# A recurrence and a gated feed-forward in one kernel: another order of the opening, the range guard moved, and one input kept in 128 rows

## The chip, the cores and the metric

The kernel runs on one core of one Trainium2 chip. The metric is the device time of one execution in microseconds (us), taken as the median of several executions; lower is better. The engines are named as in the profile: PE (TensorE, the matrix engine), DVE (VectorE), ACT (ScalarE), POOL (GpSimd), SP (SyncE, which here only issues transfers). "PEld" is PE's loading of weights.

## What is computed

The reference has two parts, one after the other. The first is a linear recurrence over 768 tokens for 4 batches and 8 heads of 48 channels; the second is a feed-forward with a sigmoid gate over all 3072 tokens (384 channels in, 1536 hidden, 384 out), in float32:

```python
for t in range(S):                       # S = 768
    cur = np.einsum('bhd,bhe->bhde', u[None] * kt, vt)
    y[:, :, t] = np.einsum('bhd,bhde->bhe', rt, state + cur)
    state = wt[:, :, :, None] * state + np.einsum('bhd,bhe->bhde', kt, vt)
...
gate = 1.0 / (1.0 + np.exp(-(x @ w_gate)))
val = x @ w_val
return gate * val @ w_out                # x is y, reshaped to 3072 tokens
```

## The kernel before, in words

**Tiling.** Time is cut into six blocks of 128 tokens, and each block holds four groups, one per batch: 24 groups, numbered q = 0 to 23. For each group the recurrence is computed in closed form ("attention"): two scans over the decays on VectorE turn k and r into scaled k and r (`prep_k` L365, `prep_r` L384), matmuls make the products of k and r and the sums for the state (`pairs`, `from_state`, `sums`, `mix`), a bonus term with u runs on POOL (`bonus1` to `bonus4`), and transposes (`turn_x`) bring the result into the form x that the feed-forward reads. x is split into a high and a low part, each a tile of the type fp32r; weights and hidden values are split the same way, and three products stand for one float32 product.

**Inputs.** For each group two loads are issued on SP's queue: `pin` (`load_pin` L324: decays, k and r, one row for each of 112 lanes, 1544 words long; for group 0 in two pieces) and `tok` (`load_tok` L333: r, k and v by token, 128 rows). The weights lie in DRAM as float64 words; their 12 slices of the hidden dimension are fetched once (`fetch` L272, the tile is called wraw, a transfer of 1151.6 KB) and turned into float32 high and low parts in five operations: `w_top` on ACT (L281), `w_body` and `w_join` on DVE (L286, L290), `w_hi` on ACT (L313), `w_lo` on DVE (L316). In the text a slice is called a words, and p3, t3, w3 are the loads of pin 3, tok 3 and words 3; ub is the small load of u for all rows. The tiles pin and tok exist twice, so the load of a third group waits until the first has been used.

**The opening** is all that happens for blocks one and two: attention of groups 0 to 11 (and part of 12), all 12 words, and the feed-forward of the first two blocks, in units of half a block (256 tokens) by one slice. Its order is not written out. A planner (`Plan` L172, fed from L611 on) plays the program through at the time of building: each operation has an engine, an estimated cost, operations it must follow, buffers it takes and gives, and a rank; at each free engine the ready operation of lowest rank is emitted. The ranks of groups and words come from the list TURNS, those of the half blocks from LAGS (unit f of half block g has rank 100 + f + LAGS[g]). Loads on SP don't choose: they are emitted strictly in the order of the list COMES, and one that must wait for its buffer holds up all behind it. The costs only steer the order; on the chip semaphores decide when anything runs.

**Blocks three to six** have a fixed order (L712 to L743): for each block n, 4 times 3 steps (j, i), one for each slice f = 3j + i. A step is a gate (9 matmuls of 128x512), a value (9), and the down products of the step before (9); ACT makes the sigmoid and the high part hh, DVE the product and the low part hl. Between them lie the parts of the next block's attention, group by group, three steps to a group (`steps` L690): the step i = 1 ends with the transposes of x, the loads of the group after next and the first scan of the next. The last block (n = 5) has no attention beside it.

**The range guard.** The cheap way to turn the weights into float32 holds only within a range. So the kernel reads all weights a second time, in 36 pieces (three to a slice, 384 KB each, the tile is called seen), and ACT sums three functions of each piece (`w_guard` L301, three activations with an accumulator on L305, L306, L307). There is one buffer for the pieces: `see(g + 1)` (L294), called at the end of `w_guard(g)`, fetches the next piece on SP's queue once ACT has read the last. In blocks three to five a piece is handled in two of three steps (i = 1 and 2, right behind the sigmoid), 24 in all; the other 12 in the first six steps of block six, two in each step (one behind the sigmoid, one behind hh). `check_bounds` (L596) and `add_bounds` (L606) then turn the sums into a flag; if it were set, a slow general form would compute everything anew (`general` L49), which doesn't happen with these inputs.

Of the kernel before, what the change touches and what calls it, by code (L numbers as in the profile page):

```python
# [9 lines left out]
F32 = mybir.dt.float32  # L10
# [38 lines left out]
def general(ctx: ExitStack, tc: tile.TileContext, dec, tok, wts, u, out, ident):  # L49
# [47 lines left out]
    with tc.For_i(0, NC_) as c:  # L97
        for b in range(B):
            nc.sync.dma_start(d[:, b], decs[b, bass.ds(c, 1)].rearrange("o a w -> (o a) w"))
        with tc.For_i(0, C) as i:  # L100
# [71 lines left out]
class Plan:  # L172
# [8 lines left out]
    def run(self):  # L181
# [3 lines left out]
        while ends:  # L185
            now = min(ends)[0]
            for e in [e for e in ends if e[0] <= now]:
                ends.remove(e)
                if e[1] in self.ops:
                    for r in self.ops[e[1]][6]:  # L190
                        room[r] += 1
                    for n in left:
                        left[n].discard(e[1])
            moved = True
            while moved:
                moved = False
                for n in sorted((n for n in self.ops if n not in started and not left[n]), key=lambda n: self.ops[n][3]):
                    engine, cost, _, _, work, take, _ = self.ops[n]
                    if engine and free.get(engine, 0.0) > now or engine == "SP" and n != transfers[0]:
                        continue  # L200
                    if any(room[r] < take.count(r) for r in take):
                        continue
                    for r in take:
                        room[r] -= 1
                    if engine:
                        free[engine] = now + cost
                        ends.append((now + cost, "-" + n))
                    if engine == "SP":
                        transfers.pop(0)
                    ends.append((now + cost + (2.0 if engine == "SP" else 0.11 if engine else 0.0), n))  # L210
# [11 lines left out]
def tile_kernel(ctx: ExitStack, tc: tile.TileContext, dec: bass.AP, tok: bass.AP, wts: bass.AP, u: bass.AP, out: bass.AP):  # L222
# [101 lines left out]
    def load_pin(q):  # L324
        t = p2.tile([L, WW + 2 * NP * C], F32, tag="pin", name=f"pin{q}")
        if q == 0:
            nc.sync.dma_start(t[:, :WW], dec[place(q)][:, :WW])
            nc.sync.dma_start(t[:, WW:], dec[place(q)][:, WW:])
        else:
            nc.sync.dma_start(t, dec[place(q)])  # L330
        pin[q] = t

# [285 lines left out]

    add("ub", "SP", 0.6, [], comes["ub"], lambda: nc.sync.dma_start(ub, u.partition_broadcast(P)))
    for q in range(3 * B + 2):  # L620
        k = rank.get(f"c{q}", 99)
        add(f"pin{q}", "SP", 2.6, [], comes[f"p{q}"], load_pin, q, take=["pin"])
        add(f"tok{q}", "SP", 2.2, [], comes[f"t{q}"], load_tok, q, take=["tok"])
        if q > 3 * B:
# [4 lines left out]
        add(f"b4_{q}", "POOL", 1.45, [f"b3_{q}"], k, bonus4, q)  # L629
        add(f"pk{q}", "DVE", 2.18, [f"pin{q}"], k, prep_k, q, take=["eg"])  # L630
# [3 lines left out]
        add(f"pr{q}", "DVE", 2.12, [f"pk{q}"], k + 0.1, prep_r, q)  # L634
# [3 lines left out]
        add(f"tk{q}", "PE", 0.5, [f"pk{q}"], k + 0.1, turn_k, q, take=["bank", "kT"])  # L638
        add(f"kT{q}", "ACT", 0.52, [f"tk{q}"], k + 0.1, take_k, q, give=["bank"])
        add(f"sm{q}", "PE", 0.75, [f"kT{q}", f"tok{q}"], k + 0.15, sums, q, take=["bank", "bank"], give=["kT"])  # L640
        add(f"mid{q}", "DVE" if old else "ACT", 0.36, [f"sm{q}", old and f"fade{q}"], k + 0.12, middle, q, take=["mid"], give=["bank"])
        add(f"keep{q}", "DVE", 0.36, [f"mid{q}"], k + 0.15, keep, q, give=["bank"])
        add(f"sc{q}", "PE", 1.2, [f"pr{q}", f"mid{q}"], k + 0.2, scores, q, take=["bank", "bank", "at"], give=["pin"] + ["ready"] * old)
        add(f"m0{q}", "DVE", 0.43, [f"sc{q}"], k + 0.2, mask, q, 0)
        add(f"m1{q}", "DVE", 0.43, [f"m0{q}"], k + 0.2, mask, q, 1)
        add(f"mx{q}", "PE", 0.85, [f"m1{q}"], k + 0.3, mix, q, give=["at"])
# [4 lines left out]
        add(f"tx{q}", "PE", 0.42, [f"y1{q}", q % B and f"tx{q - 1}"], k + 0.4, turn_x, q, take=["bank"] + ["x"] * first, give=["bon"])  # L651
        add(f"xh{q}", "ACT", 0.68, [f"tx{q}"], k, take_x, q)
        add(f"xl{q}", "DVE", 0.57, [f"xh{q}"], k, rest_x, q, give=["bank"])
        add(f"tok{q}done", None, 0, [f"mx{q}", f"sm{q}", f"b4_{q}", q % B and f"tok{q - 1}done"], k, give=["tok"])
    for f in range(NFF):
        k = rank[f"w{f}"]
        add(f"words{f}", "SP", 4.1, [], comes[f"w{f}"], fetch, f)
        add(f"wg{f}", "ACT", 1.29, [f"words{f}"], k, w_top, f)
        add(f"wb{f}", "DVE", 0.83, [f"words{f}", f and f"wb{f - 1}"], k, w_body, f, take=["full"])
        add(f"wt{f}", "DVE", 1.39, [f"wb{f}", f"wg{f}"], k, w_join, f)  # L660
        add(f"wh{f}", "ACT", 1.15, [f"wt{f}"], k, w_hi, f)
        add(f"wl{f}", "DVE", 1.4, [f"wh{f}"], k, w_lo, f, give=["full"])
    for g, (n, i0, i1) in enumerate(GROUPS):
# [50 lines left out]
    for n in range(2, NC_):  # L714
        for j in range(B):
            trio = steps((n + 1) * B + j) if n + 1 < NC_ else nothing
            for i in range(3):
# [12 lines left out]
                hidden_hi(*a)  # L730
                if n == NC_ - 1 and j < 2:
                    w_guard(guarded)
# [49 lines left out]
```

## Time and profile before

| | |
|---|---|
| median of 3 timed runs | 596.22 us (596.21 to 597.75) |
| the profiled execution, its own time | 599.11 us |
| its span, first to last instruction | 597.3 us |
| mean granted clock of PE | 0.994 |
| busy: PE, DVE, ACT, POOL | 557.5, 320.1, 248.1, 96.0 us |
| bytes read and written in DRAM | 59.26 MB, 4.72 MB |

The profile is of one execution. Busy time is that of an engine's own instructions; the same time can be busy on several engines. For each instruction the trace knows what ended the idle time before it (a matmul of PE, a landed transfer, ...), and the "chain that ended last" follows these back from the end: whatever stands in the chain held up the end. A group row of the view by stretches gives the busy time of each engine in a stretch of the span, with the number of instructions in brackets. In the view of instructions in order of time, each row is the start, the length, engine, line and operation, the tile written, an arrow and the tiles read. Names of tiles as above; sg, hh, hl are the hidden values of a step, pg, pu, po the banks of gate, value and down products, pa, pv, pk, px those of attention.

### The profile page before, as it was taken

What the parts mean: (1) busy time and instruction counts of PE and PEld (TensorE: products, weight loads), DVE (VectorE), ACT (ScalarE), POOL (GpSimd) and SP (SyncE); (2) the same over time, 40 slices, a digit from 0 to 9 for tenths busy, and PEclk for the clock granted to TensorE, in tenths of its full rate; (3) what the DMA queues carried; (4) which work ended last, traced back from release to release, by engine and by line L of the source; (5) the groups of instructions that cost most, each with busy time, mean ns of one, the idle gap of its engine ahead of it and who ended that gap; (6) DMA issues with size and microseconds to landing.
All of it is one profiled execution on the core that took longest, in us unless ns stands there. A gap on an engine that the chain in (4) does not pass through costs nothing.

```text
span 597.3 us, 14497 instructions
## 1 busy us (share of the span) xinstructions
PE 557.5 (93%) x6330; PEld 478.3 (80%) x6330; DVE 320.1 (54%) x561; ACT 248.1 (42%) x577; POOL 96.0 (16%) x86
## 2 busy tenths in 40 slices
PE   3469899999999999899999999999999999988996
PEld 2358899999999999788888888888888888866785
DVE  3887988885458736254454454454454453111222
ACT  2455455443234213343443543443544343656411
POOL 3321502012111303011220220220220210000000
PEclk9999999999999999899999999999999999999998
DMA  8993609204331242143043243043244111333001
GB/s 228 289 325 113 245 28 314 71 3 126 100 91 47 87 136 67 54 140 112 30 140 115 80 140 114 27 140 115 86 134 115 43 38 38 126 102 105 27 1 57
DMA packets 16803, 64.95 MB, mean 109 GB/s; under 512 B 1904, under 2 KB 3312, under 8 KB 15200
## 3 DMA queue, kind: packets, MB, share of 16 engines
q1 hardware_dynamic: 14000, 59.66, 32.6%
q10 hardware_dynamic: 2736, 4.33, 2.0%
q8 instruction: 51, 0.84, 0.6%
q14 instruction: 16, 0.13, 0.1%
HBM read 59.26 MB, written 4.72 MB: 107 GB/s over the span
## 4 chain that ended last, share of the span: by engine, by line
PE 76%; DMA 13%; DVE 4%; ACT 4%; issue 1%; POOL 1%; ACTq 0%; SPq 0%; DVEq 0%; POOLq 0%
PE pu L523 22%; PE pg L523 21%; PE po L576 15%; PE po L558 6%; DMA seen<-wts 5%; DMA wraw<-wts 4%; PE pa L490 3%; DMA pin<-dec 3%; PE pa L419 2%; PE pa L429 2%; PE pk L402 1%; ACT sq L305 1%; PE pv L466 1%; PE px L502 1%; DVE full L290 1%
## 5 line engine op out<-in xcount | busy, mean ns | idle before, releaser
L523 PE MATMUL pg<-x,w 128*128 128x256 f32 (+1 forms) x864 | 170.0, 342 | 4.9 <-ACT sg L534 4.8
L523 PE MATMUL pu<-x,w 128*128 128x256 f32 (+1 forms) x864 | 172.2, 344 | 0.0
L523 PEld LDWEIGHTS pg<-x,w 128*128 128x128 f32 x864 | 137.7, 192 | 25.1 <-ACT sg L534 7.3
L523 PEld LDWEIGHTS pu<-x,w 128*128 128x128 f32 x864 | 136.9, 191 | 17.6 <-DVE sg L541 0.2
L541 DVE TENSOR_TENSOR sg<-pu,sg 128x256 f32<-128x256 f32 (+1 forms) x96 | 53.4, 557 | 137.7 <-PE pu L523 114.0
L534 ACT ACTIVATE sg<-pg 128x256 f32<-128x256 f32 (+1 forms) x96 | 46.9, 488 | 128.7 <-PE pg L523 126.8
L545 ACT CAST hh<-sg 128x256 fp32r<-128x256 f32 (+1 forms) x96 | 49.2, 512 | 107.9 <-DVE sg L541 107.2
L576 PE MATMUL po<-hh,w 128*128 128x512 f32 x288 | 89.3, 392 | 0.0
L549 DVE TENSOR_TENSOR hl<-sg,hh 128x256 fp32r<-128x256 f32 (+1 forms) x96 | 57.0, 594 | 52.3 <-ACT hh L545 52.2
L363 POOL TENSOR_TENSOR bon<-tok,a 128x384 f32<-128x384 f32 x24 | 33.2, 1382 | 247.3 <-DVE a L359 247.3
L576 PEld LDWEIGHTS po<-hh,w 128*128 128x128 f32 x288 | 54.0, 188 | 10.8
L576 PE MATMUL po<-hl,w 128*128 128x512 f32 x144 | 58.8, 408 | 0.6 <-DVE hl L549 0.5
L352 POOL TENSOR_TENSOR bon<-tok,ub 128x384 f32<-128x384 f32 x24 | 33.6, 1400 | 143.2 <-DMA tok<-tok 54.9
L558 PE MATMUL po<-w,hh 128*128 128x384 f32 x192 | 48.9, 336 | 0.0
L497 DVE TENSOR_TENSOR bon<-pa,bon 128x192 f32<-128x192 f32 x48 | 15.5, 353 | 52.5 <-PE pa L490 52.3
L558 PE MATMUL po<-w,hl 128*128 128x384 f32 x96 | 33.6, 350 | 4.9 <-DVE hl L549 4.9
L397 ACT ACTIVATE junk<-eg 112x1032 bf16<-112x1032 f32 x24 | 25.5, 1064 | 26.6 <-DVE eg L387 26.5
L370 DVE TENSOR_TENSOR_SCAN eg<-pin,ends 112x516 f32<-112x516 f32 x24 | 31.2, 1298 | 9.5 <-DMA pin<-dec 9.5
L558 PEld LDWEIGHTS po<-w,hh 128*128 128x128 f32 x192 | 34.9, 188 | 0.0
L576 PEld LDWEIGHTS po<-hl,w 128*128 128x128 f32 x144 | 27.0, 188 | 7.7 <-DVE hl L549 2.4
L387 DVE TENSOR_TENSOR_SCAN eg<-pin,heads 112x516 f32<-112x516 f32 x24 | 29.9, 1246 | 0.0
L355 POOL TENSOR_TENSOR bon<-bon,tok 128x384 f32<-128x384 f32 x24 | 27.2, 1132 | 1.8
(73 smaller groups left out, 545.2 us busy)
## 6 DMA issues: line engine op xcount, KB each, us to landing
pin<-dec SPq DMA_DIRECT2D x23, 675.5 KB, 6.5
tok<-tok SPq DMA_DIRECT2D x24, 576.0 KB, 6.2
seen<-wts SPq DMA_DIRECT2D x36, 384.0 KB, 3.1
wraw<-wts SPq DMA_DIRECT2D x12, 1151.6 KB, 13.9
y<-o ACTq DMA_DIRECT2D x10, 256.0 KB, 2.0
y<-o ACTq DMA_DIRECT2D x8, 192.0 KB, 1.9
pin<-dec SPq DMA_DIRECT2D x1, 448.0 KB, 3.6
y<-o SPq DMA_DIRECT2D x1, 256.0 KB, 2.3
```

The costliest lines, as they stand in the source:

```text
L352: nc.gpsimd.tensor_tensor(out=bon[q], in0=tk[q][:, 0:DM], in1=ub, op=ALU.mult)
L355: nc.gpsimd.tensor_tensor(out=bon[q], in0=bon[q], in1=tk[q][:, DM:2 * DM], op=ALU.mult)
L363: nc.gpsimd.tensor_tensor(out=by_head(bon[q]), in0=by_head(tk[q][:, 2 * DM:]), in1=a0, op=ALU.mult)
L370: nc.vector.tensor_tensor_scan(out=e[:, 516:0:-1], data0=t[:, 516:0:-1], data1=ends[:, 516:0:-1], initial=0.0, op0=ALU.mult, op1=ALU.add,)
L387: nc.vector.tensor_tensor_scan(out=e[:, WW:WW + 516], data0=t[:, 0:516], data1=heads[:, 0:516], initial=0.0, op0=ALU.mult, op1=ALU.add,)
L523: nc.tensor.matmul(t, lhsT=w[f][:, cols], rhs=x[n][:, a, k, i0 * C:i1 * C], start=k == 0 and j == 0, stop=k == NKT - 1 and j == 2)
L534: nc.scalar.activation(sg, hid["g", n, f, i0], AF.Sigmoid)
L541: nc.vector.tensor_tensor(out=sg, in0=hid["u", n, f, i0], in1=sg, op=ALU.mult)
L545: nc.scalar.copy(hh, hid["s", n, f, i0])
L549: nc.vector.tensor_tensor(out=hl, in0=hid["s", n, f, i0], in1=hid["hi", n, f, i0].bitcast(F32), op=ALU.subtract)
L558: nc.tensor.matmul(po[n, i][:, :DM], lhsT=h[:, c], rhs=w[f][:, 2 * DM:], start=f == 0 and j == 0, stop=f == NFF - 1 and j == 2,)
L576: nc.tensor.matmul(po[n, k], lhsT=w[f][:, cols], rhs=h, start=f == 0 and j == 0, stop=f == NFF - 1 and j == 2)
```

## The change

Three edits, in one diff.

1. The opening's lists are other ones: TURNS, COMES, LAGS, and some of the planner's estimated costs (u 1.4 and not 0.6, pin 2.9 and not 2.6, words 3.7 and not 4.1, matmul work of the first three groups dearer, and others by a few hundredths). The engines' work in the opening is the same, in another order.
2. The range guard: in blocks three to five one piece in each of the 36 steps, behind hh; none in block six. The two steps that turn the sums into the flag move from slices 6 and 8 of block six to slices 0 and 3.
3. The array with decays, k and r has 128 rows for each group and not 112 (rows 112 to 127 are never used), and the tile pin and its load have 128 partitions; all that computes uses the first 112 as before.

```diff
-TURNS = "c5 c7 w10 c0 w8 w9 c1 c3 c8 w4 c4 w1 w7 w5 c11 w2 c6 c12 c10 w11 w6 c2 w0 w3 c9"
-COMES = "p0 t0 ub w0 p1 w1 t1 t3 p3 w2 w3 p2 w10 t2 w4 w5 t8 t4 w7 p4 w6 t5 w8 p5 w11 w9 p8 t6 t7 p6 t11 p7 t9 p9 p10 p11 t10 p13 t13 p12 t12"
+TURNS = "w10 c0 w6 c2 w1 c3 w0 c8 w3 c4 c1 c9 w7 c11 c7 w2 c6 w8 w11 w4 w5 c5 c12 c10 w9"
+COMES = "p0 t0 p1 ub w0 p2 t1 w1 t2 p3 w2 w3 w6 t3 w5 w4 w11 p4 t4 p5 w9 p6 t7 w7 t5 w10 w8 t6 t8 p7 p11 p8 t9 t11 p12 p9 p10 t10 t12 p13 t13"
-LAGS = [138.0, 318.0, 326.5, 116.0]
+LAGS = [96.5, 328.5, 417.5, 78.5]
...
     def load_pin(q):
-        t = p2.tile([L, WW + 2 * NP * C], F32, tag="pin", name=f"pin{q}")
+        t = p2.tile([P, WW + 2 * NP * C], F32, tag="pin", name=f"pin{q}")
...
-        pin[q] = t
+        pin[q] = t[:L]
...
                 sigmoid(*a)
-                if n < NC_ - 1 and i or n == NC_ - 1 and j < 2:
-                    w_guard(guarded)
-                    guarded += 1
...
                 hidden_hi(*a)
-                if n == NC_ - 1 and j < 2:
+                if n < NC_ - 1:
                     w_guard(guarded)
                     guarded += 1
...
-                if n == NC_ - 1 and j == 2 and i == 0:
+                if n == NC_ - 1 and j == 0 and i == 0:
                     check_bounds()
-                if n == NC_ - 1 and j == 2 and i == 2:
+                if n == NC_ - 1 and j == 1 and i == 0:
                     add_bounds()
...
-    dec = np.zeros((NG, L, WW + 2 * NP * C), np.float32)
-    dec[:, :, :NP * W1].reshape(NG, L, NP, W1)[..., 1:] = lanes(inputs["w"], 1.0)
+    dec = np.zeros((NG, P, WW + 2 * NP * C), np.float32)
+    for p in range(NP):
+        dec[:, :L, p * W1 + 1:(p + 1) * W1] = lanes(inputs["w"], 1.0)[:, :, p]
```

More of the change, by code (lines that the diff above doesn't have):

```diff
@@ L209, in run @@
                         transfers.pop(0)
-                    ends.append((now + cost + (2.0 if engine == "SP" else 0.11 if engine else 0.0), n))
+                    ends.append((now + cost + (2.0 if engine == "SP" else 0.13 if engine else 0.0), n))
                     started.add(n)
@@ L617, in add @@
         plan.add(name, engine, cost, after, rank, f and (lambda: f(*args)), take, give)
-    add("ub", "SP", 0.6, [], comes["ub"], lambda: nc.sync.dma_start(ub, u.partition_broadcast(P)))
+    add("ub", "SP", 1.4, [], comes["ub"], lambda: nc.sync.dma_start(ub, u.partition_broadcast(P)))
     for q in range(3 * B + 2):
         k = rank.get(f"c{q}", 99)
-        add(f"pin{q}", "SP", 2.6, [], comes[f"p{q}"], load_pin, q, take=["pin"])
-        add(f"tok{q}", "SP", 2.2, [], comes[f"t{q}"], load_tok, q, take=["tok"])
+        add(f"pin{q}", "SP", 2.9, [], comes[f"p{q}"], load_pin, q, take=["pin"])
+        add(f"tok{q}", "SP", 2.3 + 1.4 * (not q), [], comes[f"t{q}"], load_tok, q, take=["tok"])
         if q > 3 * B:
@@ L629, in tile_kernel @@
         add(f"b4_{q}", "POOL", 1.45, [f"b3_{q}"], k, bonus4, q)
-        add(f"pk{q}", "DVE", 2.18, [f"pin{q}"], k, prep_k, q, take=["eg"])
+        add(f"pk{q}", "DVE", 2.2, [f"pin{q}"], k, prep_k, q, take=["eg"])
         old = q >= B
@@ L637, in tile_kernel @@
             continue
[L638 removed]
+        add(f"tk{q}", "PE", 0.4 + 0.5 * (q < 3), [f"pk{q}"], k + 0.1, turn_k, q, take=["bank", "kT"])
         add(f"kT{q}", "ACT", 0.52, [f"tk{q}"], k + 0.1, take_k, q, give=["bank"])
[L640 removed]
+        add(f"sm{q}", "PE", 0.7 + 0.5 * (q < 3), [f"kT{q}", f"tok{q}"], k + 0.15, sums, q, take=["bank", "bank"], give=["kT"])
         add(f"mid{q}", "DVE" if old else "ACT", 0.36, [f"sm{q}", old and f"fade{q}"], k + 0.12, middle, q, take=["mid"], give=["bank"])
         add(f"keep{q}", "DVE", 0.36, [f"mid{q}"], k + 0.15, keep, q, give=["bank"])
[L643 removed]
+        add(f"sc{q}", "PE", 1.2 + 1.2 * (q < 3), [f"pr{q}", f"mid{q}"], k + 0.2, scores, q, take=["bank", "bank", "at"], give=["pin"] + ["ready"] * old)
         add(f"m0{q}", "DVE", 0.43, [f"sc{q}"], k + 0.2, mask, q, 0)
         add(f"m1{q}", "DVE", 0.43, [f"m0{q}"], k + 0.2, mask, q, 1)
[L646 removed]
+        add(f"mx{q}", "PE", 0.92 + 0.7 * (q < 3), [f"m1{q}"], k + 0.3, mix, q, give=["at"])
         add(f"mid{q}done", None, 0, [f"sc{q}", f"keep{q}"], k, give=["mid"])
@@ L650, in tile_kernel @@
         first = q % B == 0
-        add(f"tx{q}", "PE", 0.42, [f"y1{q}", q % B and f"tx{q - 1}"], k + 0.4, turn_x, q, take=["bank"] + ["x"] * first, give=["bon"])
+        add(f"tx{q}", "PE", 0.34 + 0.45 * (q < 3), [f"y1{q}", q % B and f"tx{q - 1}"], k + 0.4, turn_x, q, take=["bank"] + ["x"] * first, give=["bon"])
         add(f"xh{q}", "ACT", 0.68, [f"tx{q}"], k, take_x, q)
-        add(f"xl{q}", "DVE", 0.57, [f"xh{q}"], k, rest_x, q, give=["bank"])
+        add(f"xl{q}", "DVE", 0.58, [f"xh{q}"], k, rest_x, q, give=["bank"])
         add(f"tok{q}done", None, 0, [f"mx{q}", f"sm{q}", f"b4_{q}", q % B and f"tok{q - 1}done"], k, give=["tok"])
@@ L656, in tile_kernel @@
         k = rank[f"w{f}"]
-        add(f"words{f}", "SP", 4.1, [], comes[f"w{f}"], fetch, f)
+        add(f"words{f}", "SP", 3.7 + 1.6 * (not f), [], comes[f"w{f}"], fetch, f)
         add(f"wg{f}", "ACT", 1.29, [f"words{f}"], k, w_top, f)
-        add(f"wb{f}", "DVE", 0.83, [f"words{f}", f and f"wb{f - 1}"], k, w_body, f, take=["full"])
+        add(f"wb{f}", "DVE", 0.85, [f"words{f}", f and f"wb{f - 1}"], k, w_body, f, take=["full"])
         add(f"wt{f}", "DVE", 1.39, [f"wb{f}", f"wg{f}"], k, w_join, f)
         add(f"wh{f}", "ACT", 1.15, [f"wt{f}"], k, w_hi, f)
-        add(f"wl{f}", "DVE", 1.4, [f"wh{f}"], k, w_lo, f, give=["full"])
+        add(f"wl{f}", "DVE", 1.42, [f"wh{f}"], k, w_lo, f, give=["full"])
     for g, (n, i0, i1) in enumerate(GROUPS):
```

8 lines of the change are left out of this document (4 added, 4 removed).

## The prediction

> **What bounds the kernel now.** I read three views first: the page's busy times, a table of the busy time of every engine by stretches of the span that I cut where the program changes its form, and the chain that ended last. The page gives
>
> ```profile
> PE 557.5 (93%) x6330; PEld 478.3 (80%) x6330; DVE 320.1 (54%) x561; ACT 248.1 (42%) x577; POOL 96.0 (16%) x86
> ```
>
> TensorE (PE) is busy for 557.5 us of 597.3 us, so nearly 40 us of it are idle. The change removes no matmul, so what it can win lies in those 40 us. The table by stretches tells where they are (columns: stretch and its length, then the busy us of PE, weight loads, DVE, ACT and POOL with counts, the granted clock, the mean busy share of the DMA engines, GB/s). The first six rows cut up the span; the last two are looked at below.
>
> ```profile
> core 0 of [0], span 597.3 us
> core 0: us, PE busy (x) PEld busy (x) DVE busy (x) ACT busy (x) POOL busy (x), PEclk, DMA share, GB/s
> 0.00:40.00 40.00, 16.63 (x339) 13.44 (x339) 27.93 (x38) 15.00 (x23) 14.51 (x23) 1.00 0.95 265
> 40.00:75.00 35.00, 32.92 (x435) 30.78 (x436) 28.62 (x48) 18.59 (x32) 10.35 (x9) 1.00 0.55 209
> 75.00:240.00 165.00, 162.70 (x2310) 155.39 (x2310) 113.47 (x212) 61.72 (x138) 28.21 (x23) 1.00 0.32 97
> 240.00:510.00 270.00, 267.74 (x2922) 218.12 (x2921) 131.46 (x232) 114.43 (x285) 42.91 (x31) 0.99 0.30 93
> 510.00:559.00 49.00, 44.59 (x187) 33.98 (x186) 8.70 (x13) 30.70 (x88) 0.00 (x0) 1.00 0.33 105
> 559.00:598.00 39.00, 32.96 (x146) 26.55 (x144) 9.95 (x21) 7.69 (x13) 0.00 (x0) 0.95 0.07 22
> 93.00:99.00 6.00, 6.00 (x47) 6.00 (x46) 4.46 (x8) 2.65 (x5) 2.34 (x3) 1.00 1.02 267
> 99.00:102.00 3.00, 2.81 (x21) 2.60 (x21) 2.96 (x7) 1.22 (x2) 0.00 (x0) 1.00 0.99 415
> ```
>
> PE idles 40.00 - 16.63 = 23.4 us in the first 40, where the DMA engines are busy 0.95 of the time: the opening waits for data. From 40 to 240 it idles 2.1 + 2.3 us and from 240 to 510 (blocks three to five) 2.3 us: these are bound by PE. From 510 to 559, the first half of the last block, 4.4 us are idle again. The rest is the way out at the end, which the change leaves alone. So there are two places to win: the opening, and the last block's first half. The chain of the last block says what holds the second (start, length, what):
>
> ```profile
> 502.83 2.04 PE pg L523 x9
> ...
> 508.96 2.05 PE pg L523 x9
> ...
> 541.03 0.64 ACT sq L305 x2
> 541.69 2.94 DMA seen<-wts
> ...
> 558.63 2.34 PE pg L523 x9
> ```
>
> Here the chain has left PE and runs in a ring: ScalarE reads a piece of the weights for the range guard (sq), frees its one buffer, the next piece is fetched (seen), ScalarE reads that.
>
> **The guard.** One turn of the ring is 0.64 + 2.94 us and some 0.1 us of handing over, 3.7 us, and the last block asks for two turns in each step, 7.4 us. A step of that block takes PE less. The step before it, from the gate at 502.83 to the next at 508.96, took 6.13 us, with one guard piece in it:
>
> ```profile
> 505.41 0.53 ACT L305 ACTIVATE sq<-seen 128x384 bf16<-128x384 f32 x1
> ```
>
> One piece in a step without other ScalarE work cost nothing, then. From the gate of step 0 at 508.96 to that of step 7 at 558.63 are 49.67 us for seven steps, of which seven at 6.13 are 42.9. **The loss is 6.8 us.** (The table shows only 4.4 of it as idle, because a matmul held up by its start still counts as busy.) The change takes all twelve pieces out of this block, so the ring is gone; what is late next is PE itself, at 6.13 a step. I take the whole 6.8.
>
> The twelve pieces go into blocks three to five: one in each of their 36 steps, where it was two in three. That is where they could cost. A step's tightest place is the one with the transposes of x, and ScalarE's own instructions there are (start, length, instruction, in brackets the idle time before it and who ended that):
>
> ```profile
> 280.04 0.62 ACT L545 CAST hh<-sg 128x512 fp32r<-128x512 f32 x1 [2.01 <-DVE sg L541]
> 280.57 0.48 ACT L511 ACTIVATE x<-px 128x384 fp32r<-128x384 f32 x1
> 280.95 0.19 ACT L511 ACTIVATION_READ_ACCUMULATOR x<-px 128x1 f32 x1
> 283.71 0.60 ACT L534 ACTIVATE sg<-pg 128x512 f32<-128x512 f32 x1 [2.56 <-PE pg L523]
> 284.20 0.53 ACT L305 ACTIVATE sq<-seen 128x384 bf16<-128x384 f32 x1
> ...
> 285.94 0.19 ACT L307 ACTIVATION_READ_ACCUMULATOR few<-sq 128x1 f32 x1
> ```
>
> A guard piece occupies ScalarE from 284.20 to 286.13, 1.93 us. The change puts it behind hh, which ends at 280.66; the sigmoid waits for PE until 283.71. In these 3.05 us must lie the piece and the copy of x (0.57 us to 281.14): 2.50 us, 0.55 to spare. Queued behind the piece on ScalarE are that copy, then VectorE's second part of x and the scan of the next group: they move back 1.9 us, and the PE work that uses them comes in a later step. The 3.7 us of the ring fit in any step of 6.13. On SyncE's queue each fetch of a piece still stands ahead of the loads of the next group, which now are issued some 4 us later and used a round of three steps later. Cover: PE is 267.74 of 270.00 busy there with 24 pieces. I cost it at nothing; without the cover it would be some tenths of a us a step. The sums over the guard's columns move within the last block unchanged, beside a VectorE busy 8.70 of 49.00 us: nothing.
>
> **Blocks of 128 rows.** A group's load grows from 112 to 128 rows, by 14%. What one costs in a full queue is read where the queue holds nothing else than five known transfers (issue rows of SyncE's queue; then the landing times, in us after the issue, of the first and the last of them; then the page's row for all words, with the bytes of one):
>
> ```profile
> 87.37 0.33 SPq L335 DMA_DIRECT2D tok<-tok  x1
> 87.74 1.20 SPq L274 DMA_DIRECT2D wraw<-wts  x1
> 89.04 0.38 SPq L330 DMA_DIRECT2D pin<-dec  x1
> 89.46 1.04 SPq L274 DMA_DIRECT2D wraw<-wts  x2
> 90.61 1.14 SPq L330 DMA_DIRECT2D pin<-dec  x1
> ```
>
> ```profile
> tok<-tok SPq DMA_DIRECT2D x1, 576.0 KB, 3.8
> ```
>
> ```profile
> pin<-dec SPq DMA_DIRECT2D x1, 675.5 KB, 17.4
> ```
>
> ```profile
> wraw<-wts SPq DMA_DIRECT2D x12, 1151.6 KB, 13.9
> ```
>
> From 87.37 + 3.8 = 91.2 to 90.61 + 17.4 = 108.0 the queue carried three words (wraw) and two pins in 16.8 us. At the 415 GB/s of 99 to 102 a words transfer of 1151.6 KB (1179 thousand bytes) takes 2.84 us, so 8.3 us are left for two pins, 4.15 each, where their bytes at 415 would take 1.67. While pins were under way, from 93 to 99, the engines moved 267 GB/s with the same busy share, 1.02 against 0.99: all engines were occupied, and slow. Transfers of 128 rows do not show this. No trace here shows a pin of 128 rows: its bounds are 790.5 thousand bytes at 415 GB/s, 1.90 us, and 4.15 x 128/112 = 4.74 us. I take 1.90, because every row of a 128-row transfer without pins beside it is near it: a gain of 2.25 us for each pin in a full queue, against a loss of 0.6.
>
> The Trainium skill (DMA: Bandwidth & Descriptors, "Why a DMA increments its semaphore by 16 and not by 1") speaks against the change: a transfer uses the largest number of engines up to 16 that divides its rows, and both 112 and 128 are divisible by 16, so all engines work already and 14% more bytes only take longer. The busy shares agree that all work; by this rule alone the sum would be that of rival (c) below, 591.9. The Trainium skill (SBUF — State Buffer, "Door 1: The DMA port swizzle") gives the other half: each of 16 ports serves eight fixed partitions, so by my reading sixteen shares of seven rows cross ports and shares of eight need not. The 267 against 415 speaks for that; which of the two wins is a rival below.
>
> **The opening's order.** SyncE issues strictly in the list's order. The dense work of PE begins when group 1 is done; it started after its tok landed:
>
> ```profile
> 4.45 2.40 SPq L335 DMA_DIRECT2D tok<-tok  x1
> ```
>
> ```profile
> tok<-tok SPq DMA_DIRECT2D x1, 576.0 KB, 20.4
> ```
>
> ```profile
> 38.29 0.55 DVE L515 TENSOR_TENSOR x<-px,x 128x384 fp32r<-128x384 f32 x1
> ...
> 39.91 2.29 PE L523 MATMUL pg<-x,w 128*128 128x256 f32 x9
> ```
>
> It landed at 4.45 + 20.4 = 24.85, its x was there at 38.84, the first gate began at 39.91. Ahead of this tok stood p0, t0, ub, w0, p1, w1; now p0, t0, p1, ub, w0, p2. One words less (-2.84), a faster p1 (-2.25), one pin more (+1.90): it lands 3.2 us earlier. p2 must wait until group 0's scores give back its buffer, and queued behind it on SyncE are t1, w1 and all that follows; w0 covers this wait with its 2.84 us, and if that is not enough the gain shrinks. The rest of the new order I can't work out by hand, since the planner's ranks decide at each free engine. Its worth is bounded by VectorE, which must do the scans of every group and three operations for each words: it idled 35.00 - 28.62 = 6.4 us between 40 and 75, for lack of data that will now come sooner. I take a third, 2.1 us, a choice: earlier data helps VectorE only where PE then has use for its results. With the 3.2 **the opening gives 5.3 us**, taken from PE's 23.4 + 2.1 idle. Bounds: 3.2 + 6.4 = 9.6 us of gain; and with pins of 4.74 us the tok lands -2.84 + 0.59 + 4.74 = 2.5 us later, a loss of 2.5.
>
> **Sum.** 6.8 + 5.3 = 12.1 us. The profiled execution took 599.1 us (its span of 597.3 and 1.8 around it), 2.9 above the median of the timed runs, 596.2; I take the same difference off that: **584.1 us**.
>
> **Rivals.**
> (a) The opening only exchanges idle time: VectorE, busy 28.6 of 35 us from 40 to 75, holds PE back later by what it began sooner. For it: that row. Against: the shorter queue. 596.2 - 6.8 = 589.4.
> (b) The opening gains to its bound, since VectorE finds all data waiting: 596.2 - 6.8 - 9.6 = 579.8.
> (c) More rows only take longer, as by the count of engines. The opening loses 2.5: 596.2 - 6.8 + 2.5 = 591.9. For it: equal busy shares. Against: 267 beside 415 GB/s.
> (d) Slower: a guard piece costs PE in its new place what it costs now, 6.8/12 = 0.57 us, and that 36 times, 20.5 us: 584.1 + 20.5 = 604.6. Its place is ScalarE between hh and the next sigmoid; it decides once the piece there ends over 0.55 us late in most steps, and turns the balance from 12.1/36 = 0.34 us a step. For it: pieces do cost in the last block. Against: there two turns of the ring exceeded a step, here one is shorter than it, and the step at 502.83 shows one piece at no cost.
> (e) The new ranks let words go ahead of group 1 so that the opening loses as much as the guard gives: about 596.
>
> **The numbers.** My forecast 0.50, (a) 0.20, (b) 0.13, (c) 0.09, (d) 0.04, (e) 0.04. A measurement of this kernel tells 0.3%, 1.8 us, from no change. Faster: forecast, (a), (b), (c), 0.92; within: (e) 0.04; slower: (d) 0.04. The range takes in (c) and stops just short of (b) at its far end: 578 to 592.
>
> **What would show it.** In the changed profile the steps of the last block's first half should be 6.1 us apart like the others, the chain there on PE, with no guard line after the last block begins. PE's idle time from 240 to 510 should stay near 2.3 us; over 5 us would be (d). Pins in a full queue should cost about 1.9 us and the stretch of the loads run near 400 GB/s; if the GB/s beside pins stays near 270, (c). The first gate should begin near 35 us; if it does and the time does not fall by more than 7 us, (a). The prediction is wrong if the first gate begins later than 40 us, or if PE's idle time in the first 75 us has not fallen.

## The result and the profile after

The changed kernel took 582.04 us in the median of four executions (581.37 to 582.27), beside 596.22 for the kernel before (594.00 to 597.75). The ratio is 0.976 with a 95% interval of 0.973 to 0.980: 14.2 us less, where 12.1 had been forecast. The profiled execution took 581.37 us, with a span of 579.6 and a mean granted clock of 0.999. The page's first line shows the same count of matmuls, busy for 6 us less, in a span that is 17.7 us shorter:

```profile
PE 551.4 (95%) x6330; PEld 476.2 (82%) x6330; DVE 322.8 (56%) x561; ACT 248.3 (43%) x577; POOL 100.4 (17%) x86
```

The table by stretches answers to that of before (stretch, length, busy us of PE, weight loads, DVE, ACT and POOL with counts, granted clock, DMA share, GB/s). Its cuts from 240 on are moved to where the last block now begins:

```profile
core 0 of [0], span 579.6 us
core 0: us, PE busy (x) PEld busy (x) DVE busy (x) ACT busy (x) POOL busy (x), PEclk, DMA share, GB/s
0.00:40.00 40.00, 20.49 (x391) 16.25 (x391) 33.18 (x44) 16.04 (x26) 14.78 (x23) 1.00 0.72 269
40.00:75.00 35.00, 33.75 (x533) 32.03 (x535) 30.07 (x52) 21.19 (x36) 8.92 (x6) 1.00 0.67 259
75.00:240.00 165.00, 162.92 (x2265) 155.49 (x2253) 110.21 (x206) 61.43 (x138) 33.83 (x26) 1.00 0.27 98
240.00:490.00 250.00, 250.00 (x2810) 203.43 (x2801) 127.46 (x225) 126.47 (x333) 42.88 (x31) 1.00 0.34 117
...
499.00:548.00 49.00, 49.00 (x218) 40.28 (x217) 11.99 (x23) 12.04 (x21) 0.00 (x0) 1.00 0.05 17
```

In the stretch of 49 us after the last block's first gate PE now is busy for all 49 us (before 44.59), and ACT, with no pieces to read, for 12 instead of 31. From 240 to 490 PE never idles, although ACT now reads a piece in each step. In the first 40 us PE idles 19.5 us instead of 23.4, and VectorE does 33.2 us of work instead of 27.9, with the DMA engines busy for 0.72 of the time instead of 0.95.

The chain that ended last no longer leaves PE in the last block (start, length, what):

```profile
498.39 2.04 PE pg L523 x9
...
504.51 2.04 PE pg L523 x9
...
522.87 0.12 PE total L608 x2
522.99 2.28 PE pg L523 x9
...
566.07 2.04 PE pg L523 x9
...
570.15 4.13 PE po L576 x18
```

Gates are 6.12 us apart. The sums of the guard (total) stand in the chain once, with 0.12 us, and the gate behind them is 0.24 longer. From the gate of step 0 to the last down products are 570.15 - 498.39 = 71.76 us. Before, the same distance was 78.89: 7.13 us less in the last block. Its first gate moved from 508.96 to 498.39, **10.57 us, and all of these came before block three**: block three's first down products begin at 246.87, where they began at 257.42 before, 10.55 earlier. So two places gained, the two of the prediction, but the opening gained about twice the forecast 5.3 in this pair of profiles. How much of that is the change and how much the one execution of before is a question for the experiments.

In the opening two things were foretold in numbers. Tok 1 was to land 3.2 us earlier, at 21.7. Its issue and its landing (us after the issue) are now

```profile
L335 SPq DMA_DIRECT2D tok<-tok x1: 432/432/432, 12.1 to 12.1; - x1
...
DMA to landing us min/median/max: 5.4/5.4/5.4
```

that is 17.5, and 7.4 us earlier. And yet the first gate begins where it began before (39.91 there):

```profile
39.99 2.29 PE L523 MATMUL pg<-x,w 128*128 128x256 f32 x9
```

The other number is the pin of 128 rows in a full queue. Words 11 was issued at 33.0 and pin 4 next behind it at 40.1; the rows of the two give

```profile
L274 SPq DMA_DIRECT2D wraw<-wts x1: 513/513/513, 33.0 to 33.0; - x1
...
DMA to landing us min/median/max: 19.4/19.4/19.4
```

```profile
L330 SPq DMA_DIRECT2D pin<-dec x1: 328/328/328, 40.1 to 40.1; - x1
...
DMA to landing us min/median/max: 14.2/14.2/14.2
```

They land at 52.4 and 54.3: 1.9 us for the pin, as foretold (1.90).

### The profile page after: what moved, and what is told of

Its sections match the earlier page's. It is cut to its first block, busy times and chain, and to the rows that moved or that the text cites. A ratio compares the mean times of both kernels' runs of the same rounds, so it can differ in the third digit from the quotient of the medians.

```text
span 579.6 us, 14499 instructions
## 1 busy us (share of the span) xinstructions
PE 551.4 (95%) x6330; PEld 476.2 (82%) x6330; DVE 322.8 (56%) x561; ACT 248.3 (43%) x577; POOL 100.4 (17%) x86
## 4 chain that ended last, share of the span: by engine, by line
PE 90%; DVE 6%; ACT 1%; DMA 1%; issue 1%; ACTq 0%; SPq 0%; DVEq 0%
PE pu L523 26%; PE pg L523 26%; PE po L576 17%; PE po L558 8%; PE pa L490 3%; PE pa L419 2%; PE pa L429 2%; PE pk L402 2%; PE pv L466 1%; PE px L502 1%; DMA tok<-tok 1%; PE pa L466 1%; DVE w L316 1%; DVE full L290 1%; DVE eg L370 1%
## 5 line engine op out<-in xcount | busy, mean ns | idle before, releaser
L523 PE MATMUL pg<-x,w 128*128 128x256 f32 (+1 forms) x864 | 168.0, 339 | 2.1 <-ACT sg L534 1.5
L523 PE MATMUL pu<-x,w 128*128 128x256 f32 (+1 forms) x864 | 169.8, 341 | 0.0
L523 PEld LDWEIGHTS pu<-x,w 128*128 128x128 f32 x864 | 135.2, 189 | 16.9
L363 POOL TENSOR_TENSOR bon<-tok,a 128x384 f32<-128x384 f32 x24 | 37.7, 1573 | 262.4 <-DVE a L359 262.4
L352 POOL TENSOR_TENSOR bon<-tok,ub 128x384 f32<-128x384 f32 x24 | 30.9, 1289 | 113.0 <-PE px L502 60.5
L355 POOL TENSOR_TENSOR bon<-bon,tok 128x384 f32<-128x384 f32 x24 | 29.6, 1233 | 1.8
```

Source lines behind the costliest of these rows:

```text
L352: nc.gpsimd.tensor_tensor(out=bon[q], in0=tk[q][:, 0:DM], in1=ub, op=ALU.mult)
L355: nc.gpsimd.tensor_tensor(out=bon[q], in0=bon[q], in1=tk[q][:, DM:2 * DM], op=ALU.mult)
L363: nc.gpsimd.tensor_tensor(out=by_head(bon[q]), in0=by_head(tk[q][:, 2 * DM:]), in1=a0, op=ALU.mult)
L523: nc.tensor.matmul(t, lhsT=w[f][:, cols], rhs=x[n][:, a, k, i0 * C:i1 * C], start=k == 0 and j == 0, stop=k == NKT - 1 and j == 2)
```

## The experiments

The theory after these readings: the last block's ring gave 7.1 us, the third guard piece cost nothing, and the opening gained because loads came sooner and VectorE was kept busy. Rivals: the edits need each other, or the opening's gain is an early start of group 1 alone, or that of a PE which is warm sooner, or an accident of the execution that was profiled. Ratios are to the kernel before on the same chip, with 95% intervals; microseconds are worked out from them by its median there (597.81 us for the guard, the rows, the order and both together; 597.21 for the two buffers, the repeat, group 1 and the warm PE; 596.11 for the moved gate).

**The guard's edit alone.**

```diff
-                if n < NC_ - 1 and i or n == NC_ - 1 and j < 2:
-                    w_guard(guarded)
...
-                if n == NC_ - 1 and j < 2:
+                if n < NC_ - 1:
                     w_guard(guarded)
```

> The kernel before with the range guard of the change alone (one piece in each step of blocks three to five, none in block six, the flag's sums earlier); opening and 112 rows as before. My theory: the last block loses its ring of fetch and read, and the pieces cost nothing in blocks three to five: 6.8 to 7.1 us less than before, about 589.3; gates of the last block 6.12 us apart; the opening's end unmoved. The rival (a piece costs PE 0.57 us wherever it stands) expects 36 x 0.57 = 20.5 us more than without any, so 13 to 14 us slower than before, about 610.

Measured: 589.41 us, ratio 0.986 (0.982 to 0.990), that is 8.1 us less (5.7 to 10.6). The chain of this kernel:

```profile
509.46 2.04 PE pg L523 x9
...
515.58 2.04 PE pg L523 x9
...
581.22 4.13 PE po L576 x18
```

The last block takes 581.22 - 509.46 = 71.76 us, again 7.13 less. Its first gate comes 259.2 us after the first products of k and r behind the opening (at 250.29); before these were 508.96 - 249.82 = 259.1. So the 24 pieces that became 36 cost nothing in blocks three to five, and the effect that this pair of profiles shows lies in the last block. The loss itself differs a little between executions: in the three later profiles that keep the ring (128 rows, order, both) the same distance is 79.69, 78.30 and 78.08 us.

**Two buffers for the pieces of the last block, in their old places.** From piece 25 on the pieces go by turns into two halves of a tile that is free by then, and a fetch is issued two pieces ahead.

```diff
+            if g > 24:
+                seen[g] = flat[:, g % 2 * 2 * DM:(g % 2 + 1) * 2 * DM]
...
-        see(g + 1)
+        if g < 25:
+            see(g + 1)
+        if g > 23:
+            see(g + 2)
```

> The kernel before with one thing changed: in the last block the guard's pieces have two buffers in place of one (they lie in the tile of x that is free by then), so that a piece is fetched while ScalarE reads the other. My theory, that the loss of the last block is the ring of fetch and read: ScalarE's own work in a step is 0.6 + 0.6 + two pieces of 1.93, 5.1 us, less than a step of 6.12, so nearly all of the loss goes: gates 0 to 7 in 43 to 44 us in place of 49.7, the time 6 to 7 us less than before, near guard_only. Rival, that it is ScalarE's load and its order (a piece stands ahead of hh and of the sigmoid): at most 2 us less.

Measured: 587.92 us, ratio 0.988 (0.983 to 0.994), 7.0 us less (3.8 to 10.2). With all twelve pieces still read by ACT in the last block, its chain is

```profile
502.32 2.04 PE pg L532 x9
...
508.44 2.04 PE pg L532 x9
...
551.28 2.04 PE pg L532 x9
...
574.08 4.13 PE po L585 x18
```

574.08 - 502.32 = 71.76 once more. The loss was the ring through one buffer and not ACT's reading.

The first gate of this run's last block, 502.32, is a surprise of its own: it stands 6.6 us before that of the kernel before, with an opening that has the same order and the same rows. The stretch from 10 to 40 us shows a first difference, in the profile of before and then in this one:

```profile
10.00:40.00 30.00, 14.70 (x306) 11.82 (x303) 24.10 (x33) 13.18 (x21) 11.91 (x9) 1.00 1.01 279
```

```profile
10.00:40.00 30.00, 16.08 (x309) 13.26 (x309) 26.12 (x36) 14.09 (x22) 12.55 (x9) 1.00 1.01 315
```

The queue was as full (1.01), but moved 315 GB/s instead of 279, VectorE did 2 us more, and the first gate began at 37.81, 2.1 us sooner. The rest lies in the pace of PE. In the profile of before the value behind the first gate and the next gate are as slow as the first gate itself:

```profile
44.02 2.29 PE L523 MATMUL pu<-x,w 128*128 128x256 f32 x9
46.10 2.04 PE L523 MATMUL pg<-x,w 128*128 128x256 f32 x9
```

Here the same two take 1.33 us (at 41.38) and 1.24 (at 42.55), 1.8 us less together, and at the opening's end one value takes 2.30 us where it took 3.80, of which more below. With the 2.1 these are 5.4 of the 6.6 us. So the kernel before is not the same in every execution: all but two of its executions lie between 591.2 and 599.8 us, all of the changed kernel's between 581.4 and 582.9. Why the queue's rate differs was not found, and that the rate brings the earlier gate is not shown.

**128 rows alone.**

```diff
-        t = p2.tile([L, WW + 2 * NP * C], F32, tag="pin", name=f"pin{q}")
+        t = p2.tile([P, WW + 2 * NP * C], F32, tag="pin", name=f"pin{q}")
```

> The kernel before with pins of 128 rows and nothing else changed. My theory (a pin of 112 rows holds up all 16 engines, one of 128 does not): a pin in a full queue costs about 1.9 us in place of 4.2, the loads of the first 45 us move at 400 GB/s or more in place of 280, and the opening ends 2 to 5 us sooner: 591 to 594. Rival, only bytes count: a pin costs 4.7, the loads are 0.5 us later for each pin, the time is 596 to 598. Second rival: loads are faster, but VectorE decides in the opening and the time does not move by over 1 us.

Measured: 591.95 us, ratio 0.993 (0.989 to 0.996), 4.5 us less (2.6 to 6.3). Tok 1 landed at 19.3 instead of 24.85, and from 10 to 40 us the queue moved 378 GB/s with a share of 0.97. The rows win by themselves: rival (c), that more rows only take longer, falls. The profiled execution is the slowest of the eleven, 597.28 us, so its profile shows the faster loads (the first gate begins at 36.8) and not the whole gain: its last block begins at 506.36, 2.6 us sooner than before.

**The new order alone, with 112 rows.** The lists and the planner's costs are those of the changed kernel.

```diff
-TURNS = "c5 c7 w10 c0 w8 w9 c1 c3 c8 w4 c4 w1 w7 w5 c11 w2 c6 c12 c10 w11 w6 c2 w0 w3 c9"
+TURNS = "w10 c0 w6 c2 w1 c3 w0 c8 w3 c4 c1 c9 w7 c11 c7 w2 c6 w8 w11 w4 w5 c5 c12 c10 w9"
...
-LAGS = [138.0, 318.0, 326.5, 116.0]
+LAGS = [96.5, 328.5, 417.5, 78.5]
```

> The kernel before with the new lists and planner's costs, at 112 rows, guard as before. If the gain of the opening is the order's alone (first rival), 5 to 8 us less, 588 to 591. If it needs the faster pins, since the new order puts three pins ahead of tok 1 (my theory), 0 to 3 us less, and tok 1 lands 2 us later than before or about as late (24 to 27 us) in place of 17.5.

Measured: 590.80 us, ratio 0.990 (0.987 to 0.994), 5.8 us less (3.8 to 7.8). The order was expected to be worth little without the faster pins, and tok 1 to land at 24 to 27; it was worth about as much as they, and tok 1 landed at 18.6, 6.3 us sooner than before, with pins of 112 rows. The gain is not the first gate: that began at 41.6, 1.7 later than before. What changed is the stretch behind it (two rows of this kernel's table):

```profile
0.00:40.00 40.00, 18.88 (x355) 14.72 (x358) 31.16 (x43) 14.29 (x23) 15.23 (x23) 1.00 0.71 241
40.00:75.00 35.00, 34.41 (x540) 32.31 (x536) 31.23 (x51) 22.08 (x37) 9.85 (x6) 1.00 0.76 256
```

PE is busy 34.4 of the 35 us (before 32.9), and VectorE has done 62.4 us of work by 75 (before 56.6).

**Rows and order together, the old guard.** The two edits above in one kernel.

```diff
-LAGS = [138.0, 318.0, 326.5, 116.0]
+LAGS = [96.5, 328.5, 417.5, 78.5]
...
-        pin[q] = t
+        pin[q] = t[:L]
```

> The change without its guard part. The opening is then that of the changed kernel: 7 us less than before in timed runs (589), and the last block keeps its ring with a loss of 6.8 to 7.1 us. If the parts add up, this and guard_only together give the 14.2 us of the whole change; if the sum falls short by over 2 us, one part changes what the other is worth.

Measured: 588.64 us, ratio 0.987 (0.983 to 0.991), 7.9 us less (5.7 to 10.2). The two parts overlap (4.5 + 5.8 alone). With the guard's 8.1 the parts give 16.0, beside 14.2 for the whole, which is within their intervals. Its last block begins at 499.28, between the 498.39 and 499.6 of the changed kernel's two profiles, so the third guard piece shows no cost in the new order either.

**The changed kernel once more**, on the chip of the next three.

> The changed kernel itself once more, on the chip and beside the runs on which the three kernels sent with it are measured: about 582, in a spread of 1 to 2 us, where the kernel before spreads over 5 us or more. If the wider spread of the kernel before comes from a pause of PE of over 2 us at the end of its opening, after which the clock is sometimes halved for some us, the changed kernel, which has no such pause, shows no halving before the very end.

Measured: 582.43 us, ratio 0.978 (0.974 to 0.983), that is 12.9 us less (10.0 to 15.8). Its last block begins at 499.6, its first gate at 40.9, and its clock is whole from 45.8 us to the very end.

**Group 1 ahead.** In the changed kernel, group 1's rank is put before the words and groups that had overtaken it.

```diff
-TURNS = "w10 c0 w6 c2 w1 c3 w0 c8 w3 c4 c1 c9 w7 c11 c7 w2 c6 w8 w11 w4 w5 c5 c12 c10 w9"
+TURNS = "w10 c0 c1 w6 c2 w1 c3 w0 c8 w3 c4 c9 w7 c11 c7 w2 c6 w8 w11 w4 w5 c5 c12 c10 w9"
```

> The changed kernel with group 1 ranked right behind group 0 in TURNS, all else equal, so that the first half block can begin as soon as group 1's tok is there. As the prediction put it (PE's dense work begins with group 1, and its start sets the opening): first gate at 28 to 32 us in place of 40, the time 5 us or more less than the changed kernel. Rival, that VectorE's work as a whole decides (it is 9.3 to 9.9 of 10 us busy from 10 to 40 in the changed kernel) and what is done early for one group is missing for the others: the first gate as early, the time within 2 us of the changed kernel, in either direction.

Measured: 591.72 us, ratio 0.992 (0.989 to 0.995), that is 9.3 us more than the changed kernel, which neither the theory nor its rival had foreseen. The first gate did begin sooner, at 37.4 (28 to 32 was expected), and VectorE was no less busy, but PE pays behind it:

```profile
40.00:75.00 35.00, 30.50 (x518) 27.42 (x518) 31.13 (x49) 21.15 (x36) 9.31 (x6) 1.00 0.54 217
```

30.5 us busy of 35, where the changed kernel has 33.75. 4.2 us of PE's waits in this stretch are for VectorE. So an early first gate was worth nothing here, since the work behind it ran dry. The reading that fits is that what counts is what VectorE has ready when PE asks for the next thing, over the whole stretch to 75 us and beyond; the rows to 75 show about a third of the 9.3 us.

**PE kept warm.** In the changed kernel, 70 matmuls 128x384 of zeros (bf16) stand ahead of the PE work of groups 0 and 1.

```diff
+            nc.tensor.matmul(idle[:, :DM], lhsT=cold[:, :P], rhs=cold, start=True, stop=True, skip_group_check=True)
```

> The changed kernel with 70 matmuls of 128x384 on zeros added ahead of PE's operations of groups 0 and 1, into a bank that is not yet used, and nothing else changed. In the changed kernel the first gate takes 2.22 us for nine matmuls that later take 1.08, and the matmuls of groups 0 and 1 take about twice what later ones do, all while the records show a granted clock of 1.00. If this is PE's slow state after idle time, the added matmuls bring it to full speed early: the first gate takes about 1.1 us, the matmuls of groups 0 and 1 half as long. If the chain of these groups decides, the time falls by 2 to 4 us; if VectorE decides, it stays within 1 us. If the doubled times come from something else, nothing shortens and the time is the same or up to 2 us longer.

Measured: 581.86 us, ratio 0.978 (0.973 to 0.983), like the changed kernel. The first gate's nine matmuls took 1.34 us where they take 2.29, so PE was quicker in the opening, and nothing came of it: in the new order, PE's own pace there is covered, by VectorE as it seems, which is busy 28.06 of the 30 us from 10 to 40. The old order, in which PE stays slow for longer, was not tried with a warm PE.

**A gate moved into the pause at the opening's end.** The profile of before has one long pause of PE, and slow matmuls behind it (start, length, instruction, in brackets the idle time before it):

```profile
234.59 2.35 PE L523 MATMUL pg<-x,w 128*128 128x512 f32 x9 [0.53 <-ACT sg L534]
...
244.51 0.44 PE L558 MATMUL po<-w,hl 128*128 128x384 f32 x1 [2.27 <-DVE hl L549]
...
246.10 3.80 PE L523 MATMUL pu<-x,w 128*128 128x512 f32 x9
```

```profile
245.00:250.00 5.00, 5.00 (x28) 3.92 (x30) 0.00 (x0) 1.98 (x4) 0.00 (x0) 0.66 0.22 79
```

After the pause of 2.27 us the granted clock was 0.66 in the mean of the next 5 us, and a value of 128x512 took 3.80 us. The planner has put the first gate of block three (pg 128x512) at 234.59, ten us ahead, and nothing is left for the pause. The edit makes that gate wait in the planner for the last products of the opening:

```diff
-    add("ahead", "PE", 2.1, [f"xl{2 * B + i}" for i in range(B)] + ["pg2_11", "pg3_11"], 200, gate, *ahead, take=["pg"])
+    add("ahead", "PE", 2.1, [f"xl{2 * B + i}" for i in range(B)] + ["pg2_11", "pg3_11", "pu2_11", "pu3_11"], 200, gate, *ahead, take=["pg"])
```

> The kernel before with one operation of PE later in the order: the first gate of block three (nine matmuls 128x512) also waits, in the planner, for the last products of the opening, so that it falls into the pause at the opening's end (2.27 us at 242.2 in the profile of before, followed by a granted clock of 0.50 until 249.85). If that pause and the halved clock are part of what the old order costs: no pause over 1 us and no granted clock under 1 between 235 and 255, and a time 2 to 5 us below before. If the gate's place doesn't matter, because PE then waits for the gate's successors instead: within 1 us of before.

Measured: 593.73 us, ratio 0.995 (0.992 to 0.998), 3.2 us less (1.5 to 4.8). The same place in its profile:

```profile
239.48 2.25 PE L523 MATMUL pg<-x,w 128*128 128x512 f32 x9
241.91 0.44 PE L558 MATMUL po<-w,hl 128*128 128x384 f32 x1 [0.18 <-DVE hl L549]
...
243.38 2.30 PE L523 MATMUL pu<-x,w 128*128 128x512 f32 x9
```

The pause is 0.18 us and the value takes 2.30. So the place of one operation, at the other end of the opening than the prediction looked at, is worth about 3 us in the old order. The changed kernel has no such pause either. Its gate stands near the opening's end, and the value follows in 2.32 us:

```profile
233.10 2.25 PE L523 MATMUL pg<-x,w 128*128 128x512 f32 x9
...
237.00 2.32 PE L523 MATMUL pu<-x,w 128*128 128x512 f32 x9
```

**Two more profiles of the kernel before.** The kernel was not edited.

> The kernel before once more, for its profile. If the halved clock behind the pause at the opening's end belongs to its order: a pause of over 1.5 us between 235 and 250 again, and where the clock after it is granted whole, a span some 2.5 us shorter than 597.3. If the pause came by chance in that one execution: no such pause.

> As the run before this one: a third profile of the kernel before. With a pause of 2.0 us or more a halved clock for some 5 us, without it none; the span differs between the profiles by about the 2.5 us that nine products of 512 columns then took longer.

Measured: 598.85 and 598.21 us. Both show the pause (2.26 us) and then a granted clock of 0.50 for 3.4 us, so they don't show the same kernel with the clock whole. The profile with the guard's edit alone, which has the old opening, does: the same pause, and the value behind it in 2.29 us.

```profile
246.59 0.44 PE L558 MATMUL po<-w,hl 128*128 128x384 f32 x1 [2.26 <-DVE hl L549]
...
248.07 2.29 PE L523 MATMUL pu<-x,w 128*128 128x512 f32 x9
```

The profiles with two buffers and with 128 rows agree (a pause of 2.26, a value of 2.30). So the pause belongs to the order, and the halved clock follows it in some executions only: 3.80 - 2.29 = 1.5 us in the execution of before that was profiled. Which ones can be read off the traces, and stands at the end.

**Loads alone.** All computation is left out. Seven series of ten loads, each row 6176 bytes; VectorE reads a word of each load as it lands.

```diff
+    for s, rows in enumerate((112, 128, 120, 96, 112, 128, 64)):
+        for i in range(10):
+            nc.sync.dma_start(t[:rows], dec[i, :rows])
```

> Transfers alone; the whole computation is left out and zeros are written. Seven series of ten loads each of 6176 bytes a row, of 112, 128, 120, 96, 112, 128 and 64 rows, every series waited for. If rows that are no multiple of 128 cost what the full queue of before seemed to show: about 4.1 us a load at 112 rows (170 GB/s) and 1.9 at 128 (415 GB/s). If a load costs by its bytes: 1.67 us at 112 rows and 1.90 at 128, both at 415 GB/s; then the slow pins were due to something beside them.

Measured (the start of VectorE's reading is the landing; first 128 rows, then 120, 96, 112 and 64; of 128, 96 and 112 rows the rows shown are eight loads apart, of 120 seven, of 64 three):

```profile
36.56 0.15 DVE L236 TENSOR_TENSOR zero<-zero,r128x 64x1 f32<-64x1 f32 x1 [1.72 <-DMA r128x<-dec]
...
51.69 0.15 DVE L236 TENSOR_TENSOR zero<-zero,r128x 64x1 f32<-64x1 f32 x1 [1.73 <-DMA r128x<-dec]
...
58.68 0.15 DVE L236 TENSOR_TENSOR zero<-zero,r120x 64x1 f32<-64x1 f32 x1 [6.84 <-DMA r120x<-dec]
...
82.29 0.15 DVE L236 TENSOR_TENSOR zero<-zero,r120x 64x1 f32<-64x1 f32 x1 [3.19 <-DMA r120x<-dec]
...
95.63 0.15 DVE L236 TENSOR_TENSOR zero<-zero,r96x 64x1 f32<-64x1 f32 x1 [6.79 <-DMA r96x<-dec]
...
113.99 0.15 DVE L236 TENSOR_TENSOR zero<-zero,r96x 64x1 f32<-64x1 f32 x1 [2.11 <-DMA r96x<-dec]
...
122.42 0.15 DVE L236 TENSOR_TENSOR zero<-zero,r112x 64x1 f32<-64x1 f32 x1 [6.67 <-DMA r112x<-dec]
...
144.47 0.15 DVE L236 TENSOR_TENSOR zero<-zero,r112x 64x1 f32<-64x1 f32 x1 [2.55 <-DMA r112x<-dec]
...
174.58 0.15 DVE L236 TENSOR_TENSOR zero<-zero,r64x 64x1 f32<-64x1 f32 x1 [4.99 <-DMA r64x<-dec]
...
180.29 0.15 DVE L236 TENSOR_TENSOR zero<-zero,r64x 64x1 f32<-64x1 f32 x1 [1.76 <-DMA r64x<-dec]
```

| rows | us a load | GB/s |
|---|---|---|
| 128 | 15.13 / 8 = 1.89 | 418 |
| 120 | 23.61 / 7 = 3.37 | 220 |
| 112 | 22.05 / 8 = 2.76 | 251 |
| 96 | 18.36 / 8 = 2.30 | 258 |
| 64 | 5.71 / 3 = 1.90 | 208 |

Neither expectation holds. Loads of 112 rows are slow by themselves, with nothing beside them, so it is their form and not their company; but one costs 2.76 us (2.59 in the first series) and not 4.15.

## Why the prediction was right, and where it was wrong

**The guard: right, in mechanism and size.** Forecast 6.8 us, measured 7.13 against the profile of before in each of three profiles without the ring: pieces moved away (twice), and a second buffer. Against all four profiles with the ring it is 6.3 to 7.9. "I cost it at nothing", of the third piece in blocks three to five, held: PE is busy 250.00 of 250.00 us there, and with the guard's edit alone the last block comes as long after the opening as before (259.2 and 259.1 us). Rival (d) fell with that.

**128 rows: the forecast price right, the price of before wrong.** 1.90 us was taken for the pin of 128 rows, 1.9 was measured in the queue and 1.89 alone. But the 4.15 for 112 rows charged the two pins with all the time that five loads took beyond 2.84 us a words. Alone such a load takes 2.6 to 2.8; the rest of the two times 4.15, some 3 us over three words, is the queue's: words that ran slower beside pins, or pins beside words. The landings of before point to the words: words 0, with pin 1 queued behind it, landed at 15.9, 5.5 us after ub, where the sum gave a words 2.84. So the sum for tok 1 came out short (7.4 us sooner, not 3.2). It counted one faster pin, although pin 0 stands ahead of tok 1 as well, and took one words less for 2.84. Either edit alone brought tok 1 forward by more than that sum: the rows by 5.6 us, the order by 6.3.

The Trainium skill (SBUF — State Buffer, "Door 1: The DMA port swizzle") makes the bandwidth of a transfer a matter of how many of the 16 ports its partitions reach, and by its table partitions 0 to 63 reach eight. The loads alone agree: 64 rows take the 1.90 us of 128. By the same table 112 rows fill no port beyond its eight partitions and would take 1.9 us too (an estimate from the table and the 1.89 of 128 rows), and the measured 2.76 says that the ports alone don't give the price. The prediction's reading, that shares of seven rows cross ports and shares of eight need not, fits 112 and 128 rows; but 120 rows, which are fifteen shares of eight, were the slowest of all at 3.37. What makes the form slow stays open.

**The opening: the sign right, its step wrong.** The step that failed is "the dense work of PE begins when group 1 is done", with tok 1's landing as what moves it and "the first gate should begin near 35 us". The text called itself wrong if that gate began later than 40; it began at 39.99, and at 40.9 in the second profile, so by its own sign this step failed. Tok 1 landed 7.4 us earlier and group 1 got nothing of it: the new ranks let words and groups 2 and 3 pass it on a VectorE that was busy 28.65 of the 30 us from 10 to 40. With group 1 put first again the first gate came 2.6 us sooner than in the changed kernel's first profile, and the kernel got 9.3 us slower. The first gate was a milestone, not what limits the opening.

What replaces it, in the two profiles: PE waits less later on, and is slow for a shorter time. From the two tables, PE's idle time fell by 3.86 us in the first 40, by 0.83 up to 75, and by 0.22 up to 240; the pause of 2.27 us at the opening's end went, and with it the 1.5 us (3.80 - 2.32) that a halved clock had cost the value behind it. These are 8.7 of the 10.57 us. Most of the other 1.9 is busy time of a slow PE. The rows of before with 2.29 and 2.04 us are, in the changed kernel,

```profile
42.07 1.37 PE L523 MATMUL pu<-x,w 128*128 128x256 f32 x9
...
44.18 1.33 PE L523 MATMUL pg<-x,w 128*128 128x256 f32 x9
```

which is 1.6 us less. The slow stretch ends where a trace's first record of the granted clock begins (the views show 1.00 ahead of it, too): at 47.91 us before, 8.0 after the first gate, and at 42.37 now, 2.4 after it (8.7 and 8.8 in the other two profiles of before, 4.9 in the other of the changed kernel). Which share of this sum is the order's and which the rows' is not separated. The 2.1 us that the prediction gave to "VectorE must do the scans" was the right kind of term in the wrong place: VectorE did 5.2 us more in the first 40, which the prediction hadn't counted, and 1.5 more from 40 to 75.

**The size.** In the timed runs the opening gave about 14.2 - 7.1 = 7.1 us, 12.9 - 7.1 = 5.8 in the repeat, or 7.9 with rows and order alone, between the forecast 5.3 and the 9.6 of rival (b). The 10.57 of the profiles is more, since the profiled execution of before took 599.11 us, 2.9 above the median, and that of after 0.7 below its own; subtracting the 2.9 from the sum was the right way to treat it. So the total came out close by a sound term for the guard and by luck for the opening: its 5.3 was near what was measured, but came from a landing that moved no gate and from a third of VectorE's idle time, taken as a choice.

**Open:** why the old queue's rate differs between executions (279 to 315 GB/s in six profiles of the old order with 112 rows), why 112 and 120 rows are slow, and what a PE that is warm sooner would win in the old order. What each of the other entries of the new lists gives wasn't tried.

## What to carry to other kernels

Read a ring of fetch and use through one buffer as one number, compare it with the step beside which it runs, and move it to where the step is longer: this part was told to about a us. An opening that a planner orders can't be priced by when one early result is ready: ask of each order where the bottleneck engine will wait later, up to the last pause before the regular part, and fill that pause with work that is ready anyway. Busy time doesn't show a slow engine: compare what the same group of matmuls takes. And when a queue is full but slow, suspect the form of a load before its bytes: here 14% more bytes took nearly a third less time (1.89 us and 2.76).

## What the runs showed of the hardware

- Time of a load from the same array against its rows is not monotone: 1.90 us for 64, 2.30 for 96, 2.76 for 112, 3.37 for 120, 1.89 for 128.
- A pause of PE of 2.26 us was followed by a granted clock of 0.50 in three profiles with the old opening (all of the kernel before), and by a whole clock in three others with that pause (guard's edit, two buffers, 128 rows). The Trainium skill (TensorE: Matmul & The Clock Gate, "Part 1: The HAM clock gate (the "warmup" mystery)") says that the clock is halved after an idle window of about 3.4 us, and that the window runs freely, so that its effect differs from run to run. The second part agrees with these runs; as to the first, pauses of 2.26 us were enough.
- When it follows can be worked out from the clock records of the traces. In all thirteen profiles with the whole computation the clock is halved only a whole number of steps of 3.413 us after the trace's first clock record, and a halved stretch within the work lasts one step. In the three profiles of before it begins 58 steps behind that record, at 245.9, 245.5 and 245.8 us, and PE had been idle for 2.04, 2.26 and 2.23 us of the step that ended there. In the three others a step's end cuts the pause: at most 1.81, 1.45 and 1.70 us of it lie in one step. Over all thirteen, every halving follows a step with at least 1.93 us of idle PE, and no step with 1.81 or less is followed by one. So what counts in these traces is not the pause's length alone but how it lies to the steps. This is read from the traces and was not tried by an edit.
- In the opening the granted clock reads 1.00 while nine matmuls 128x256 take 2.29 us; with dummy matmuls ahead of them they take 1.34. The clock column doesn't show that PE is slow there, since the first clock record of these traces comes later (42.37 us in the changed kernel's); the length of a known group of matmuls does.
